# Twenty-nine input loads go out of ScalarE's DMA queue, a pair's turned r is copied at once, and every list of the schedule is new

## The chip, the cores and the metric

The kernel runs on one core of one Trainium2 chip. The metric is the device time of one execution in microseconds (us), the median of several runs. The core has five engines that run side by side, each working through its own list of instructions in order: TensorE (PE, matmul), VectorE (DVE), ScalarE (ACT), GpSimd (POOL) and SyncE (SP), which here only issues DMAs. Sixteen DMA engines move data between HBM and SBUF. TensorE writes to PSUM, which has eight banks.

## The reference

Two stages, one after the other. The first is a linear attention with a state per head (batch 4, 8 heads, 768 tokens, head size 40):

```python
for t in range(S):
    y[:, :, t] = np.einsum('bhd,bhde->bhe', rt, state)
    Sa = np.einsum('bhde,bhe->bhd', state, at)
    state_decay = state * wt[:, :, None, :] - np.einsum('bhd,bhe->bhde', Sa, bt)
    state = state_decay + np.einsum('bhd,bhe->bhde', vt, kt)
```

The second mixes tokens and channels of x, which is y with its heads side by side (4 x 768 x 320):

```python
theta = x @ w_theta
zr, zi = x * np.cos(theta), x * np.sin(theta)
y = np.einsum('ts,bsd->btd', w_tok_r, zr) + np.einsum('ts,bsd->btd', w_tok_i, zi)
u = x + y
return u + np.maximum(u @ w_ch, 0.0)
```

## The kernel before

**Tiling.** The tokens are cut into chunks of 128: six chunks a batch, 24 in all, named i = 0 to 23. Within a chunk the recurrence is turned into matrix products over the 128 tokens, with all 8 heads side by side (320 columns). Each chunk needs six inputs of 160 KB: w, k, b, a, v and r. `loads` (lines 433 to 449) issues them: one DMA a chunk for w, k, b and a (line 436), one for v from chunk 8 on, and two DMAs a pair of chunks for r, and for v below chunk 8 (line 448). These are 144 DMAs, and SP issues all of them in the kernel before.

**A chunk's stages.** `prep` takes ln(w) on ACT (line 472), sums it over the tokens on PE, takes exponentials on ACT (496, 506, 514), scales k, b and a by them on POOL (line 456, tiles kb and ah), and turns kb, ah, v and r (token to feature) on PE, by `turned` (lines 404 and 408) and `turn_runs` (569 and 572). A turned tile goes to PSUM and is copied to SBUF on ACT or DVE (lines 422 and 426 for most; 584 and 586 for r). `scores` (603, 612, 614) makes four 128 x 1024 score tiles a chunk, masked on DVE, or copied by ACT and masked on POOL. `recurrence` and `readout` follow (lines 640 to 842). `theta` and `sines` give cos and sin, `sines` multiplies them with x on POOL (line 894, zr and zi), `mix_row` does the token mixing (line 910: 288 matmuls of 320 columns), and `channels` the last product and the store (946, 949). Matrix weights are loaded by POOL (lines 961 and 989).

**Two ways to turn a tile.** In one bank: each 128 x 128 block is one transpose of 128 columns (lines 404, 569). In two banks: each block is two transposes of 64 rows and 64 columns, one for the upper and one for the lower half of the partitions, each into its own bank (lines 408, 572). `split` tells which of the two a tile has; the copies out of PSUM read the same number of elements either way.

**What sets the order.** Every step is an operation in a `Plan`, numbered in the order in which the program adds it. The list `ORDER` says in which order all are issued, and thereby each engine's own order. An operation can have a second variant: on another engine, or for a turned tile the one in two banks; `PICK` names the operations that take it. `HOMES` gives, in that order, the PSUM bank of each tile. `WARM` puts matmuls on constant data ahead of a few operations. The lists are constants of the program. Waits follow from the data: an engine waits at an operation until what it reads is there and what it overwrites has been read, and everything behind it in that engine's list waits too.

**A pair's r.** `turn_runs` turns r of two chunks in one PSUM tile. Before, two ACT copies of 128 x 256 words take it out, one a chunk (lines 581 to 588, 24 copies in all).

Of the kernel before, what the change touches and what calls it, by code (L numbers as in the profile page):

```python
# [9 lines left out]
FP32 = mybir.dt.float32  # L10
# [209 lines left out]
def kernel(  # L220
# [14 lines left out]
    nc = tc.nc  # L235
# [840 lines left out]
```

## Time and profile before

| | before |
|---|---|
| time, median of 3 runs | 197.25 us (196.4, 197.25, 198.79) |
| span of the profiled execution, first to last instruction | 195.9 us |
| PE / DVE / ACT / POOL busy | 94% / 83% / 77% / 74% of the span |
| granted TensorE clock, mean | 0.997 |
| first issue of an input load / issue of the last one | 0.81 us / 151.8 us |

The profile's span leaves out what lies ahead of the first and behind the last instruction; the three runs lie 0.5 to 2.9 us above it, their median 1.35 us. A PE that is busy all the time may still not be at its peak, since the ends of matmuls are modelled.

### The profile page before, as it was taken

To read this page: it belongs to the slowest core of one execution; us is meant where nothing else is said; L and a number is where in the kernel's file an instruction comes from. 1 tells how busy PE (TensorE), PEld (TensorE's weight loads), DVE (VectorE), ACT (ScalarE), POOL (GpSimd) and SP (SyncE) were. 2 spreads that over 40 slices of the span, in tenths; PEclk is the share of its full clock that TensorE was granted. 3 is DMA by queue.
4 is the path that set the end of the run, shared out by engine and by line. 5 is a ranking of instruction groups with operands and counts; after the bars stand their busy time and mean duration, and the time that the engine had idled before them with its cause. 6 is when DMAs were issued, how large, how long until landed. Compare 5 with 4: busy or idle time off the path is not lost.

```text
span 195.9 us, 8473 instructions
## 1 busy us (share of the span) xinstructions
PE 184.3 (94%) x3516; PEld 145.4 (74%) x3516; DVE 163.3 (83%) x260; ACT 150.6 (77%) x336; POOL 145.1 (74%) x211
## 2 busy tenths in 40 slices
PE   7889899999997999999899999999999999999992
PEld 6767687887786778887577787887788768767661
DVE  5378799999998999898897999999999938664453
ACT  3575879799997997999689599979999867575111
POOL 8367466579969999696699959868879997469100
PEclk9999999999999999999999999999999999999998
DMA  5999897999999999979999997789899977535055
GB/s 118 217 205 182 148 214 157 174 171 206 216 183 166 197 180 185 225 122 200 179 183 158 166 200 129 164 147 180 161 178 203 168 172 102 128 136 74 32 197 172
DMA packets 134646, 32.78 MB, mean 167 GB/s; under 512 B 124816, under 2 KB 134608, under 8 KB 134608
## 3 DMA queue, kind: packets, MB, share of 16 engines
q1 hardware_dynamic: 131680, 29.19, 76.6%
q0 software_dynamic: 2784, 2.97, 9.3%
q8 instruction: 27, 0.44, 0.9%
q10 hardware_dynamic: 144, 0.08, 0.1%
q14 instruction: 11, 0.09, 0.1%
HBM read 29.54 MB, written 3.93 MB: 171 GB/s over the span
## 4 chain that ended last, share of the span: by engine, by line
PE 61%; DMA 12%; POOL 9%; ACT 6%; DVE 4%; SPq 4%; issue 2%; ACTq 0%; DVEq 0%; POOLq 0%
PE banks L910 16%; PE banks L603 9%; PE banks L404 8%; PE banks L792 5%; DMA raw_a<-in_a_dram 4%; DMA raw_kb<-in_k_dram 4%; SPq L436 3%; PE banks L408 3%; DMA uT<-up 2%; PE banks L569 2%; PE banks L663 2%; POOL kb L456 2%; PE banks L686 2%; PE banks L802 2%; DMA raw_v<-in_v_dram 2%
## 5 line engine op out<-in xcount | busy, mean ns | idle before, releaser
L456 POOL TENSOR_TENSOR kb<-raw_kb,ex 128x320 bf16<-128x320 f32 x46 | 37.1, 814 | 8.0 <-DMA raw_kb<-in_k_dram 3.0
L910 PE MATMUL banks<-zr,wtok_r 128*128 128x320 bf16 x144 | 41.0, 300 | 0.2
L910 PE MATMUL banks<-zi,wtok_i 128*128 128x320 bf16 x144 | 40.8, 299 | 0.1
L456 POOL TENSOR_TENSOR ah<-raw_a,we 128x320 bf16<-128x320 f32 x22 | 19.0, 865 | 12.9 <-ACT we L506 4.7
L612 DVE TENSOR_TENSOR lamu<-banks,mask_p 128x1024 bf16<-128x1024 f32 x22 | 26.8, 1219 | 1.5 <-PE banks L603 0.8
L612 DVE TENSOR_TENSOR psi<-banks,mask_p 128x1024 bf16<-128x1024 f32 x22 | 26.8, 1219 | 0.8 <-PE banks L603 0.7
L612 DVE TENSOR_TENSOR phi<-banks,mask_n 128x1024 bf16<-128x1024 f32 x18 | 21.9, 1216 | 1.6 <-POOL r L462 1.3
L612 DVE TENSOR_TENSOR lamv<-banks,mask_p 128x1024 bf16<-128x1024 f32 x17 | 20.7, 1219 | 1.6 <-PE banks L603 1.0
L894 POOL TENSOR_TENSOR zi<-cs,xp 128x320 bf16<-128x320 f32 x22 | 17.2, 791 | 2.0 <-ACT cs L879 1.2
L910 PEld LDWEIGHTS <-wtok_r 128*128 128x128 bf16 x144 | 14.0, 97 | 5.6 <-issue 0.3
L603 PE MATMUL banks<-aT,kbT 64*128 64x128 bf16 x384 | 17.2, 217 | 0.9 <-DVE kbT L426 0.3
L894 POOL TENSOR_TENSOR zr<-cs,xp 128x320 bf16<-128x320 f32 x22 | 17.4, 802 | 0.1
L910 PEld LDWEIGHTS <-wtok_i 128*128 128x128 bf16 x144 | 14.0, 98 | 3.8 <-issue 0.3
L829 PE MATMUL banks<-kb,lamv 128*128 128x40 bf16 x192 | 14.9, 180 | 0.0
L831 PE MATMUL banks<-kb,lamu 128*128 128x40 bf16 x192 | 14.8, 179 | 0.0
L603 PEld LDWEIGHTS <-kbT 64*128 64x128 bf16 x384 | 11.8, 94 | 3.7 <-ACT kbT L422 1.1
L829 PEld LDWEIGHTS <-lamv 128*128 128x128 bf16 x192 | 13.2, 96 | 0.4
L916 DVE TENSOR_TENSOR up<-banks,xp 128x320 bf16<-128x320 f32 x22 | 10.6, 485 | 3.1 <-PE banks L910 2.9
L831 PEld LDWEIGHTS <-lamu 128*128 128x128 bf16 x192 | 13.0, 96 | 0.0
L472 ACT ACTIVATE lw<-raw_w 128x320 bf16<-128x320 f32 x24 | 11.5, 477 | 1.5 <-DMA raw_w<-in_w_dram 1.3
L496 ACT ACTIVATE ex<-banks 128x328 f32<-128x328 f32 (+1 forms) x24 | 10.8, 450 | 2.2 <-PE banks L491 1.1
L822 PE MATMUL banks<-gd,rT 128*128 128x80 bf16 x80 | 12.2, 197 | 0.0
(202 smaller groups left out, 583.0 us busy)
## 6 DMA issues: line engine op xcount, KB each, us to landing
raw_w<-in_w_dram SPq DMA_DIRECT2D x24, 160.0 KB, 4.3
raw_v<-in_v_dram SPq DMA_DIRECT2D x24, 160.0 KB, 3.7
raw_a<-in_a_dram SPq DMA_DIRECT2D x24, 160.0 KB, 3.9
raw_kb<-in_k_dram SPq DMA_DIRECT2D x24, 160.0 KB, 4.2
raw_kb<-in_b_dram SPq DMA_DIRECT2D x24, 160.0 KB, 4.2
raw_r<-in_r_dram SPq DMA_DIRECT2D x24, 160.0 KB, 3.8
out_dram<-oo SPq DMA_DIRECT2D x9, 160.0 KB, 2.6
wrow_i<-in_moe_w_tok_i_dram POOLq DMA_DIRECT2D x6, 192.0 KB, 5.3
```

What stands on the lines that cost most here:

```text
L404: nc.tensor.transpose(out=t[:, m * 128:m * 128 + 128], in_=src, identity=ident)
L456: pool = ("POOL", lambda: nc.gpsimd.tensor_tensor(out=dst, in0=in0, in1=in1, op=ALU.mult))
L472: add("ACT", "ln", i, lambda: nc.scalar.activation(out=paired(lw)[:, :, :, 0:D], in_=paired(raw_w[s4]), func=AF.Ln), 473, [("raw_w", s4)], ...
L496: got = add("ACT", "exp", i, lambda: nc.scalar.activation(out=ex[:, :, 0:D] if no_total else ex.rearrange("p h x -> p (h x)"), in_=sums(ps ...
L603: nc.tensor.matmul(t[:, q, g, :], lhsT=lhs[g][rows(q)], rhs=rhs[g][rows(q)], start=True, stop=True)
L612: add("DVE", kindm, i, lambda: nc.vector.tensor_tensor(out=flat, in0=whole(), in1=mask.to_broadcast([128, 2 * G, 128]), op=ALU.mult), 1217 ...
L822: nc.tensor.matmul(t[:, g * 80:g * 80 + 80], lhsT=by_two(rT)[g], rhs=gd[:, 2 * g:2 * g + 2, :], start=True, stop=False, skip_group_check=True)
L829: nc.tensor.matmul(o, lhsT=lamv[:, p, g, :], rhs=kb[:, 0, h, 0:D], start=first, stop=False, skip_group_check=True)
L831: nc.tensor.matmul(o, lhsT=lamu[:, p, g, :], rhs=kb[:, 1, h, 0:D], start=False, stop=True, skip_group_check=True)
L894: pool = ("POOL", lambda: nc.gpsimd.tensor_tensor(out=dst, in0=in0, in1=in1, op=ALU.mult))
L910: nc.tensor.matmul(acc(), lhsT=wtok[nm][j][:, s], rhs=zs[c][:, s], start=n == 0 and c == 0, stop=n == NT - 1 and c == 1)
L916: add("DVE", "uadd", q, lambda: nc.vector.tensor_tensor(out=u, in0=acc(), in1=x, op=ALU.add), 488, [pk, x_key(q)], [u_key(q)], at="row")
```

## The change

Three edits to the program, and new lists.

1. `loads` gives each of the 144 load operations a second variant, the same DMA issued by ACT (`nc.scalar.dma_start`).
2. In `turn_runs`, the two ACT copies of a pair's r become one of 128 x 512 words that writes both chunks' halves. There are 12 operations fewer (1602 become 1590), so all numbers behind them shift.
3. `ORDER`, `HOMES`, `PICK` and `WARM` are new as a whole.

Decoded against the numbering of the operations, the new lists say this (i in brackets):

| | before | after |
|---|---|---|
| loads issued by ACT | 0 | 29: a x9 (0, 4, 10, 11, 13, 14, 15, 17, 19), w x8 (1, 3, 4, 5, 6, 8, 17, 20), b x4 (1, 9, 17, 20), early v x3, k x2 (6, 8), r x2 (0), v x1 (17) |
| tiles kb turned in two banks | 8 of 23 | 21 of 23 (new: 0 to 5, 8, 9, 10, 12, 15, 21, 22) |
| nu | 2 of 22 | 12 of 22 |
| ah / v, early v, v back | 7, 5 | 10, 7 |
| u and x, feature-major | 1 and 5 | 7 and 9 |
| r (of 12) | 6 | 8 |
| turned tiles in two banks, all | 39 | 79 |
| planned operations: ACT / DVE / POOL / SP | 326 / 235 / 186 / 180 | 339 (29 of them loads) / 237 / 189 / 151 |

Of the ACT operations that change sides: copies of kb on DVE go from 7 to 4 and of ah from 8 to 5, copies `nx` on DVE from 4 to 8, early v from 0 to 4; casts of v on ACT go from 5 to 2 (POOL 11 to 14); z products on DVE from 2 to 6 (POOL 46 to 42); score tiles on ACT are 17 before, 18 after. The first chunks' loads of ACT stand in its list between its early operations: `la0, ln0, lw1, r, ew0, exp0, r, ea0, lb1, ln1, ...`. `lk8` stands ahead of `ln8`, `la13` ahead of the copy `ekb12`. At `spsi8`, `spsi13`, `spsi16` and `spsi23` (the first score of those chunks) PE has 0, 24, 48 and 90 of its 144 pairs of token-mixing matmuls behind it in the old order, 0, 24, 48 and 93 in the new one; at `y23`, the last readout, 106 in both.

```diff
@@ loads
         for key, dst, src in load(i):
-            add("SP", "l" + key[0][4:], i,
-                lambda dst=dst, src=src: nc.sync.dma_start(out=dst, in_=src),
-                600, [], [key], work=1030)
+            by = [(e, lambda q=q, dst=dst, src=src: q.dma_start(out=dst, in_=src))
+                  for e, q in (("SP", nc.sync), ("ACT", nc.scalar))]
+            add("SP", "l" + key[0][4:], i, by[0][1], 600, [], [key], work=1030, alts=(by[1],))
...
-                add("SP", "load" + nm, i, lambda c=c, to=raw[s], runs=runs: nc.sync.dma_start(
-                    out=to[:, c], in_=runs[c]), 600, [], [run_key(nm, i, c)], work=520)
+                by = [(e, lambda q=q, c=c, to=raw[s], runs=runs: q.dma_start(
+                    out=to[:, c], in_=runs[c])) for e, q in (("SP", nc.sync), ("ACT", nc.scalar))]
+                add("SP", "load" + nm, i, by[0][1], 600, [], [run_key(nm, i, c)], work=520,
+                    alts=(by[1],))
@@ turn_runs
-        for x, (dst, dkey) in enumerate(dsts):
-            if nm != "r":
+        if nm != "r":
+            for x, (dst, dkey) in enumerate(dsts):
                 evac("ACT", "e" + nm, i + x, pr, dst, 512, [dkey], x)
-                continue
-
-            def words(x=x, dst=dst):
-                out = dst.bitcast(FP32)
-                if split(pr):
-                    nc.scalar.copy(out=out, in_=ps(pr)[:, x, 0:256])
-                    return
-                nc.scalar.copy(out=out.rearrange("p (a n) -> p a n", a=2), in_=ps(pr).rearrange(
-                    "p (a n) -> p a n", a=2)[:, :, 128 * x:128 * x + 128])
-            add("ACT", "e" + nm, i + x, words, 512, [pr], [dkey])
+            return
+        both = rT_t[i // 2 % 3].rearrange("p x n -> p (x n)").bitcast(FP32)
+
+        def words():
+            if split(pr):
+                nc.scalar.copy(out=both.rearrange("p (x n) -> p x n", x=2), in_=ps(pr)[:, :, 0:256])
+                return
+            nc.scalar.copy(out=both.rearrange("p (x a n) -> p x a n", x=2, a=2),
+                           in_=ps(pr).rearrange("p (a x n) -> p x a n", a=2, x=2))
+        add("ACT", "er", i, words, 512, [pr], [dkey for _, dkey in dsts])
@@ the lists
-WARM = {21: (0, 25), 30: (1, 4), 33: (2, 1), 28: (1, 8), 41: (1, 11)}
+WARM = {21: (5, 25), 33: (1, 1), 30: (3, 4), 28: (5, 8), 41: (0, 11)}
...
```

249 rows, old and new, of tables (HOMES, ORDER, PICK) are left out of this document.

## The prediction

> **What bounds the kernel now.** I read the page's busy line first, then the windows (busy time in stretches of the span), the chain that ended last, and SP's timeline.
>
> ```profile
> span 195.9 us, 8473 instructions
> PE 184.3 (94%) x3516; PEld 145.4 (74%) x3516; DVE 163.3 (83%) x260; ACT 150.6 (77%) x336; POOL 145.1 (74%) x211
> ...
> PE 61%; DMA 12%; POOL 9%; ACT 6%; DVE 4%; SPq 4%; issue 2%; ACTq 0%; DVEq 0%; POOLq 0%
> ```
>
> PE is busy 94% of the span and makes 61% of the chain, but the whole is no single limit. The windows show it, with start and end, length, busy time of PE, PE's weight loads, DVE, ACT and POOL (instructions), the granted clock, the DMA engines' share and GB/s:
>
> ```profile
> 0.00:20.00 20.00, 16.42 (x233) 13.68 (x235) 12.86 (x40) 10.98 (x25) 12.61 (x35) 1.00 0.93 182
> 20.00:40.00 20.00, 19.14 (x396) 15.63 (x392) 18.18 (x22) 16.72 (x44) 11.28 (x14) 1.00 0.89 175
> 40.00:60.00 20.00, 18.61 (x384) 15.11 (x382) 19.61 (x25) 18.70 (x45) 16.99 (x25) 1.00 1.04 192
> 60.00:80.00 20.00, 19.53 (x440) 15.82 (x442) 18.93 (x27) 18.00 (x41) 19.78 (x29) 1.00 1.04 183
> 80.00:100.00 20.00, 19.30 (x420) 14.88 (x413) 17.86 (x27) 17.58 (x36) 14.97 (x22) 1.00 1.00 175
> 100.00:120.00 20.00, 19.77 (x391) 15.50 (x390) 18.06 (x31) 16.74 (x39) 17.91 (x25) 1.00 0.93 170
> 120.00:140.00 20.00, 19.98 (x504) 16.27 (x502) 19.53 (x28) 18.38 (x44) 16.19 (x22) 1.00 0.89 166
> 140.00:155.00 15.00, 14.82 (x325) 12.29 (x322) 14.61 (x22) 14.44 (x35) 13.92 (x19) 1.00 0.94 188
> 155.00:170.00 15.00, 14.79 (x235) 11.14 (x233) 10.74 (x18) 10.01 (x17) 11.94 (x16) 1.00 0.76 128
> 170.00:185.00 15.00, 14.91 (x165) 10.48 (x164) 7.42 (x14) 7.63 (x15) 9.55 (x12) 1.00 0.38 93
> 185.00:196.00 11.00, 7.07 (x63) 4.64 (x61) 5.55 (x13) 1.39 (x4) 0.00 (x0) 0.93 0.47 164
> ```
>
> Three stages. Up to 100 us PE is idle 7.0 us in all (3.58, 0.86, 1.39, 0.47, 0.70) while the DMA engines are 89 to 104% busy (a share over 1 means that packets overlapped): input loads lead. From 100 to 155 us PE, DVE, ACT and DMA are all near full and PE is idle 0.4 us of 55. From 155 us on only PE is full, down to the last stores. The clock is granted in full, so it plays no part. The chain says the same of the first stage (start, length, what):
>
> ```profile
> 48.22 7.07 DMA raw_kb<-in_k_dram
> ...
> 82.25 2.88 SPq L436
> ...
> 86.11 8.33 DMA raw_a<-in_a_dram
> 94.58 0.88 POOL ah L456
> ...
> 95.50 0.29 PE banks L408 x8
> ```
>
> Two loads, k of chunk 8 and a of chunk 13, take 7 and 8 us and hold POOL, and behind it PE. In the new lists both are among the 29 of ACT.
>
> **The tiles turned in two banks.** This is the surest term. Groups by line and shape, PE matmuls (count | busy us, mean ns):
>
> ```profile
> L404 PE MATMUL banks<-wide,kb 128*128 128x128 bf16 x120 | 9.8, 225 | 1.0 <-ACT phi L614 0.7 <-POOL kb L456 0.3
> L404 PE MATMUL banks<-wide,ah 128*128 128x128 bf16 x64 | 6.4, 224 | 0.0
> L569 PE MATMUL banks<-wide,r 128*128 128x128 bf16 x48 | 3.7, 219 | 0.0
> L408 PE MATMUL banks<-wide,kb 64*128 64x64 bf16 x128 | 3.2, 191 | 0.2 <-ACT uT L422 0.2
> L572 PE MATMUL banks<-wide,r 64*128 64x64 bf16 x96 | 2.4, 190 | 0.0
> L408 PE MATMUL banks<-wide,ah 64*128 64x64 bf16 x56 | 2.0, 192 | 1.2 <-POOL ah L456 1.2
> L404 PE MATMUL banks<-wide,xp 128*128 128x128 bf16 x20 | 1.8, 218 | 0.0
> L408 PE MATMUL banks<-wide,xp 64*128 64x64 bf16 x50 | 1.6, 190 | 0.0
> ```
>
> A whole kb is 8 matmuls: 120 are 15 tiles, 9.8/15 = 0.65 us of PE each. In two banks it is 16: 128 are 8 tiles, 3.2/8 = 0.40. So a kb tile that changes saves 0.25 us. In the same way ah: 6.4/16 - 2.0/7 = 0.11; r: 3.7/6 - 2.4/6 = 0.22; x (5 blocks): 1.8/4 - 1.6/5 = 0.13. nu and v have ah's four blocks and are priced as ah, u as x, early v as r. By the decoded lists: kb +13 tiles, 3.3 us; nu, ah, v together +14 (10, 3 and 1), 1.5; u and x +10, 1.3; r and early v +3, 0.7. That is 6.8 us of PE. It isn't 6.8 us of time. By chunk numbers only three kb (15, 21, 22; 0.75), three tiles net of nu, ah and v (0.33), some nine of u and x (1.2) and one r (0.2) fall behind about 95 us, where PE is the engine that ends last: 2.4 us, taken in full. The other 4.4 lie where loads lead; they shorten links of the chain but mostly make PE wait longer. I take a fifth, **0.9** (bounds 0 and 4.4), beside the **2.4**. What hides the rest is the load stream; if that gets faster, more of the 4.4 counts. The price in banks: 40 more tiles hold two of the eight banks. No row shows PE waiting long for a bank; the kb row's 0.7 us behind an ACT copy (phi, of another tile) is nearest. I take nothing, with 2.8 us (four such waits) as the other end.
>
> **The 29 loads.** What an issue costs its engine, by SP's timeline (start, length), first to last load:
>
> ```profile
> 0.81 0.46 SPq L436 DMA_DIRECT2D raw_w<-in_w_dram  x1
> ...
> 24.92 0.53 SPq L436 DMA_DIRECT2D raw_kb<-in_k_dram  x1
> ...
> 90.50 3.70 SPq L436 DMA_DIRECT2D raw_kb<-in_b_dram  x1
> ...
> 151.08 1.34 SPq L448 DMA_DIRECT2D raw_r<-in_r_dram  x2
> ```
>
> SP issues without a pause: 144 loads and 3 stores in 151.6 us, 1.03 us each; a free issue takes 0.53, the slowest 3.70. The long ones come when SP's queue is full of transfers that the DMA engines haven't done, since these are 89% busy and more. ACT's queue would hold a fifth as many, so I price its issues near the free end, at 0.58: 29 x 0.58 = 16.8 us of ACT. Nothing in the trace shows a load on ACT; the bounds are 0.46 and 1.03 a piece, 3.70 for single ones. From 20 to 155 us ACT is idle 14.4 us, and about 20 of the 29 lie there (11.6 us), so it fits, with little left. Behind an issue in ACT's list stand copies out of PSUM for which PE waits; ACT makes 6% of the chain, so I charge 6% of 14.7 (16.8 less 2.1 saved below): **0.9 us lost**, with the rival below as the other end.
>
> What it gains: the two loads of the chain no longer stand behind SP's full queue. PE is idle 1.39 us in the stretch that holds the first wait and 0.70 in that of the second; I take half of the 2.1, **1.0**, since neither idle time is all due to them; bounds 0 and 2.1.
>
> The Trainium skill (DMA: Bandwidth & Descriptors, Issuing engines are not separate DMA queues) says that DMAs of SP, ACT and GpSimd run on the same 16 engines and that issuing from several saves issue time only. By it this 1.0 would be nothing, and the sum 195.5 us. The same page (Queues, rings and completion order) has each DMA engine go round between the queues that have work, packet by packet; by that a load on a nearly empty queue overtakes those of a full one, which speaks for the 1.0. No run here shows two loading queues yet.
>
> **The copy of r.**
>
> ```profile
> L422 ACT COPY kbT<-banks 128x512 f32<-128x512 f32 x12 | 7.1, 592 | 2.6 <-PE banks L404 2.5
> L586 ACT COPY rT<-banks 128x256 f32<-128x256 f32 x12 | 4.4, 384 | 0.2 <-PE banks L569 0.2
> L584 ACT COPY rT<-banks 128x256 f32<-128x256 f32 x12 | 4.1, 382 | 0.8 <-PE banks L572 0.8
> ```
>
> Two copies of 0.383 become one that has the size of kbT's, 0.592: 0.174 saved a pair, 2.1 us of ACT over 12. The even chunk's half is ready 0.21 us later, the odd one's 0.17 earlier. ACT doesn't end last; nothing on the path, beyond the 2.1 already set against the issues.
>
> **Work that changes engine, and the order.** Without loads ACT goes from 326 to 310 operations, of which 12 are the copies of r. DVE gets 2 more, POOL 3. At DVE's mean of 0.63 us (163.3/260) that is 1.3 us; DVE is 98% busy in 120 to 140 us, so I count half, **0.6 us lost**; POOL, 74% busy, hides its three. The new order keeps the old shape (the token mixing stands 0 to 3 pairs further at the same chunks); I give it no term.
>
> **Sum.** -2.4 - 0.9 - 1.0 + 0.9 + 0.6 = -2.8 us, 195.9 to 193.1 us of span. The median of the runs is 1.35 us above the profiled span, so about **194.5 us**, 1.4% below 197.25.
>
> **Rivals.**
>
> *The load stream stays the floor (chance 0.27).* The same 144 loads move the same bytes through DMA engines that are 89 to 104% busy until 155 us. Then all that PE saves before turns into waiting for loads, and only what lies behind 155 us counts: about seven of the changed tiles, 0.8 us, 196.4 us. The Trainium skill's rule on issuing engines (same page and section as above) leads to this case too. For it: the DMA share. Against: from 100 to 140 us it is 0.89 to 0.93, so there is some room, and a second queue that always has work can use it.
>
> *ACT becomes the bound (0.16).* If issues on ACT take what SP's do, 1.03 us, the 20 behind 20 us cost 20.6, less 1.9 for the r copies: 18.7 against 14.4 us of idle time up to 155 us. ACT then ends last, 4.3 us late: 201.5, and with copies that PE waits for about 202 us (199.5 to 205). It decides where the mean issue passes (14.4 + 1.9)/20 = 0.82 us. For it: SP's mean, and that one full DMA side may hold up both queues. Against: SP's free issues.
>
> *The second queue opens the first stage (0.17).* Early loads land sooner, the two waits go, and most of the 4.4 us of PE time and the whole 2.1 count: 3.5 + 1.1 beyond my sum is 189.9 us at best; two thirds of that way is 191.5 (189.5 to 193). For it: PE's 7.0 us of idle time before 100 us, and a chain that there runs through loads and POOL. Against: the first 20 us already move 182 GB/s.
>
> The forecast has the remaining 0.40, with a range of its own of 192 to 197.
>
> **Range and chances.** 190.5 to 199.8 holds all but the far part of ACT's case (about 0.12) and the edge of the fast one (0.05). What can be told from no change is about 2%: 193.3 and 201.2. Faster: the fast case, 0.17, and a third of the forecast's 0.40, together 0.31. Slower: some two thirds of ACT's case, 0.11, and 0.03 for bank waits beyond 2.8 us: 0.14. Within: 0.55.
>
> **What would show it.** Right: L408 kb at x336 and about 8.4 us, L404 kb at x16; ACTq load issues of about 0.6 us; waits of POOL for k and a under 2 us each; PE idle below 6 us in the first 100. ACT's idle time in 20 to 155 us should fall to some 5 us. The floor's case: the last load lands where it did and PE is idle longer between 40 and 155 us. ACT's case: issues over 0.82 us, and PE waiting for copies of ACT. Wrong altogether: PE waiting for banks, or chunk 0 later than before.

## The result, and the profile after

The changed kernel is slower: 208.16 us (median of four, 207.04 to 210.18) against 196.85 us of the kernel before on the same chip, a ratio of 1.053 with a 95% interval of 1.047 to 1.059. The forecast was 194.5 us, with a range up to 199.8. Ratios here compare undisturbed executions only; where the times of one kernel spread more than that, its range is given beside them.

The page after, with the lines that answer to those of before: span, busy time of the engines, and the chain that ended last by engine.

```profile
span 206.6 us, 8911 instructions
...
PE 183.9 (89%) x3744; PEld 142.4 (69%) x3744; DVE 164.7 (80%) x262; ACT 148.0 (72%) x320; POOL 148.1 (72%) x214
...
PE 47%; DMA 15%; POOL 8%; SPq 8%; ACT 8%; DVE 7%; issue 4%; ACTq 1%; DVEq 0%; POOLq 0%
```

PE is busy as long as before (183.9 us against 184.3), but the span is 10.7 us longer: the loss is time in which PE waits. The windows show where. The columns are start and end, length, busy time of PE, weight loads, DVE, ACT and POOL, granted clock, DMA share and GB/s.

```profile
0.00:20.00 20.00, 11.56 (x143) 9.67 (x144) 6.35 (x30) 5.56 (x11) 11.49 (x34) 1.00 1.03 188
20.00:40.00 20.00, 18.96 (x460) 14.79 (x458) 18.41 (x26) 16.77 (x39) 11.93 (x15) 1.00 1.04 187
...
60.00:80.00 20.00, 18.14 (x338) 14.25 (x337) 16.61 (x23) 15.93 (x36) 15.95 (x23) 0.91 1.07 184
80.00:100.00 20.00, 19.51 (x487) 15.38 (x485) 17.16 (x27) 18.83 (x41) 18.39 (x27) 1.00 1.18 206
100.00:120.00 20.00, 18.33 (x377) 13.59 (x370) 18.88 (x32) 14.89 (x29) 18.32 (x25) 1.00 0.66 127
120.00:140.00 20.00, 17.79 (x440) 14.14 (x440) 16.63 (x24) 16.32 (x39) 13.60 (x19) 1.00 1.03 187
```

Three stretches have lost PE time against before: the first (11.56 us busy instead of 16.42), 60 to 80 us (18.14 instead of 19.53), and 100 to 140 us (36.12 instead of 39.75). In the first two the DMA engines are at least as full as before. In 100 to 120 us they are not: 0.66 instead of 0.93. So two things are to be explained.

**The first: ACT stands still ahead of its own load issues.** ACT's timeline after (start, length, engine, line; ACTq is a DMA issue of ACT; in brackets the idle time before and what ended it):

```profile
5.87 0.44 ACT L503 ACTIVATE ex<-banks 128x328 f32<-128x328 f32 x1
8.21 0.54 ACTq L453 DMA_DIRECT2D raw_r<-in_r_dram  x1
8.79 0.37 ACT L431 COPY aT<-banks 128x256 f32<-128x256 f32 x1 [2.48 <-PE banks L413]
13.85 0.41 ACTq L440 DMA_DIRECT2D raw_kb<-in_b_dram  x1
14.30 0.47 ACT L479 ACTIVATE lw<-raw_w 128x320 bf16<-128x320 f32 x1 [5.14 <-DMA raw_kb<-in_b_dram]
```

The issues are short (0.54 and 0.41 us). But between the copy at 8.79 and the issue at 13.85 ACT does nothing for 4.7 us, and ln(w) of chunk 1 stands behind that issue. The timeline says that this ln(w) waited for a landing of `raw_kb`, a tile that it does not read. That contradiction is the clue: what waits is the DMA issue ahead of it. In the trace each DMA of SP or ACT reports its landing on one of eight semaphores (counters that an engine can wait for), which all of them share, 22 or 23 DMAs on each, whichever engine issues. Ahead of 23 of ACT's 29 issues the trace has a wait for the issue's own semaphore, so the earlier DMA on it has to land first. For b of chunk 1 that was SP's load of b of chunk 2: it landed at 13.825 us by the trace's semaphore events, and ACT's issue began 0.02 us later. Eleven of the 29 issues began within 0.1 us of such a landing. The chain that ended last goes through four of them, right behind a landing; two of the four (start, length, what):

```profile
12.87 3.16 DMA raw_r<-in_r_dram
16.05 0.55 ACTq L453
16.64 0.45 ACT ex L503
...
114.50 5.28 DMA raw_r<-in_r_dram
119.86 0.37 ACTq L440
120.27 0.59 ACT rT L591
```

Here an ACT operation on the path waits for a load that it has nothing to do with. Added up over the 29 issues, ACT stands idle 14.4 us ahead of them (4.68, 2.58, 1.90, 1.89 and 1.00 the largest). PE has its longest wait behind the first of these (what waits, for what, us in all, times, longest):

```profile
PE banks L510 <- ACT lw L479: 5.1, 1, 5.1
```

**The second: SP halts.** SP's timeline after:

```profile
100.29 0.60 SPq L440 DMA_DIRECT2D raw_kb<-in_k_dram  x1
111.78 0.55 SPq L453 DMA_DIRECT2D raw_r<-in_r_dram  x1
```

SP issues nothing for 10.9 us. The new order puts the first load of r of pair 18 right behind k of chunk 15; its buffer is that of pair 14 (two buffers), and POOL's cast of r of pair 14 ends at 111.75. In the kernel before, SP never stood over 0.9 us ahead of a load. The late load of pair 18's other half, issued at 114.50, is the one in the chain above that ACT then waits for.

The delay against before does not grow evenly: it is 4.9 us at chunk 0's first score (10.7 before, 15.5 after), falls to 3.6 by chunk 7, is 7.0 at chunk 8, 5.4 at chunk 13, 8.7 at chunk 16 and 10.4 at chunk 23. So PE makes up a part in between, and loses again behind the waits of 60 to 80 and 100 to 140 us.

### The profile page after: what moved, and what is told of

Read it like the earlier page. It is cut to its first block, busy times and chain, and to the rows that moved or that the text cites. A ratio compares the mean times of both kernels' runs of the same rounds, so it can differ in the third digit from the quotient of the medians.

```text
span 206.6 us, 8911 instructions
## 1 busy us (share of the span) xinstructions
PE 183.9 (89%) x3744; PEld 142.4 (69%) x3744; DVE 164.7 (80%) x262; ACT 148.0 (72%) x320; POOL 148.1 (72%) x214
## 4 chain that ended last, share of the span: by engine, by line
PE 47%; DMA 15%; POOL 8%; SPq 8%; ACT 8%; DVE 7%; issue 4%; ACTq 1%; DVEq 0%; POOLq 0%
PE banks L917 10%; DMA raw_r<-in_r_dram 8%; PE banks L610 7%; SPq L440 7%; PE banks L799 4%; PE banks L413 4%; PE banks L409 4%; DMA wch<-in_moe_w_ch_dram 3%; DMA raw_w<-in_w_dram 2%; POOL zr L901 2%; DMA uT<-up 2%; PE banks L693 2%; PE banks L670 2%; ACT cs L886 2%; PE banks L651 1%
## 5 line engine op out<-in xcount | busy, mean ns | idle before, releaser
L463 POOL TENSOR_TENSOR kb<-raw_kb,ex 128x320 bf16<-128x320 f32 x48 | 38.5, 812 | 9.9 <-ACT ex L503 8.3
L619 DVE TENSOR_TENSOR psi<-banks,mask_p 128x1024 bf16<-128x1024 f32 x23 | 28.0, 1219 | 10.2 <-PE banks L610 9.4
L619 DVE TENSOR_TENSOR phi<-banks,mask_n 128x1024 bf16<-128x1024 f32 x17 | 20.7, 1220 | 1.0 <-PE banks L610 0.6
L901 POOL TENSOR_TENSOR zi<-cs,xp 128x320 bf16<-128x320 f32 x20 | 16.1, 819 | 6.1 <-ACT cs L886 3.9
L619 DVE TENSOR_TENSOR lamv<-banks,mask_p 128x1024 bf16<-128x1024 f32 x16 | 19.5, 1217 | 0.7 <-PE banks L610 0.7
L610 PE MATMUL banks<-aT,kbT 64*128 64x128 bf16 x384 | 18.6, 223 | 0.8 <-ACT vT L427 0.8
L901 POOL TENSOR_TENSOR zr<-cs,xp 128x320 bf16<-128x320 f32 x19 | 15.5, 830 | 1.8 <-ACT cs L886 1.8
L708 POOL TENSOR_TENSOR gt<-sum,ex 128x320 bf16<-128x320 f32 x13 | 9.6, 739 | 9.8 <-DVE sum L704 8.6
L923 DVE TENSOR_TENSOR up<-banks,xp 128x320 bf16<-128x320 f32 x22 | 10.4, 485 | 4.5 <-PE banks L917 4.2
```

What stands on the lines that cost most here:

```text
L463: pool = ("POOL", lambda: nc.gpsimd.tensor_tensor(out=dst, in0=in0, in1=in1, op=ALU.mult))
L610: nc.tensor.matmul(t[:, q, g, :], lhsT=lhs[g][rows(q)], rhs=rhs[g][rows(q)], start=True, stop=True)
L619: add("DVE", kindm, i, lambda: nc.vector.tensor_tensor(out=flat, in0=whole(), in1=mask.to_broadcast([128, 2 * G, 128]), op=ALU.mult), 1217 ...
L708: add("POOL", "wgt", i, lambda: nc.gpsimd.tensor_tensor(out=new_state, in0=sum_t, in1=wm.to_broadcast([128, 8, D]), op=ALU.mult), 830, [(" ...
L901: pool = ("POOL", lambda: nc.gpsimd.tensor_tensor(out=dst, in0=in0, in1=in1, op=ALU.mult))
L923: add("DVE", "uadd", q, lambda: nc.vector.tensor_tensor(out=u, in0=acc(), in1=x, op=ALU.add), 488, [pk, x_key(q)], [u_key(q)], at="row")
```

## The experiments

Operations are numbers in the lists. `PICK` entries set to 1 give an operation its second variant: a load on ACT, a tile in two banks. All times are compared with the kernel before on the same chip.

**All loads back on SP**, the new order kept. The 29 load numbers leave `PICK`:

```diff
 PICK = {
-    3: 1, 4: 1, 5: 1, 8: 1, 10: 1, 18: 1, 19: 1, 25: 1, 26: 1, 27: 1, 28: 1, 30: 1, 32: 1, 33:
+    25: 1, 26: 1, 27: 1, 28: 1, 30: 1, 32: 1, 33: 1, 34: 1, 35: 1, 36: 1, 37: 1, 39: 1, 40: 1,
...
```

> The changed kernel with its 29 ACT loads issued by SP again, at the same places of the order; all else as changed. Theory A (the trace after shows ACT starting a load 20 ns after the landing of an earlier DMA on the same completion semaphore, with nothing behind it running meanwhile): nearly all of the 11 us come back, 194 to 198 us, chunk 0's first score near 10.7 us again instead of 15.5. Rival B (the new order, banks and two-bank tiles are at fault): 204 us or more. Not told apart at 199 to 203.

203.4 us, ratio 1.024 (1.015 to 1.033). About half of the loss goes and half stays, between the two expectations: the loads on ACT are not the whole cause, and the new order costs something without them. Chunk 0's first score is back at 10.4 us. SP's halt is gone as well, although the order is the same: SP has 29 issues more and comes to the load of pair 18 at 109.27 us, 0.1 us behind its issue before, when the cast of pair 14 has just ended (108.94). So this run takes away both ACT's waits and the halt, and the halt belongs to the loads on ACT: with fewer issues of its own SP is earlier at a buffer that isn't free yet.

**The first nine ACT loads back on SP** (nine numbers leave `PICK`: a of chunk 0, w of 1, 3 and 4, b of 1, both loads of r of pair 0 and of v of pair 2):

```diff
 PICK = {
-    3: 1, 4: 1, 5: 1, 8: 1, 10: 1, 18: 1, 19: 1, 25: 1, 26: 1, 27: 1, 28: 1, 30: 1, 32: 1, 33:
+    25: 1, 26: 1, 27: 1, 28: 1, 30: 1, 32: 1, 33: 1, 34: 1, 35: 1, 36: 1, 37: 1, 39: 1, 40: 1,
...
```

> The changed kernel with only the first nine of its ACT loads (those ahead of chunk 3) issued by SP, 20 still by ACT. Theory A: the 5 to 7 us that chunks 0 to 2 are late after the change come back, 201 to 204 us, and the loss behind 55 us stays. If the early loss is made up later anyway (PE has waits there), 206 to 208. Rival B: 207 to 209, chunk 0 still late.

209.9 us, 1.051 (1.038 to 1.064): nothing gained. Chunk 0's first score comes at 10.0 us, as early as before. But the next ACT loads now wait instead: w of chunk 5 2.47 us (k of chunk 4 landed at 27.255, the issue began at 27.28), a of chunk 4 1.57, and w of chunk 20 2.49 where it was 1.00. The sum is 12.6 us of ACT, little less than 14.4. Taking off the loads that waited did not take off the waiting.

**The old order with the same 29 loads on ACT**, the second variant added to `loads` as in the change:

```diff
 PICK = {
-    25: 1, 31: 1, 37: 1, 39: 1, 40: 1, 48: 1, 49: 1, 75: 1, 80: 1, 85: 1, 86: 1, 115: 1, 118: 1,
+    3: 1, 4: 1, 5: 1, 8: 1, 10: 1, 18: 1, 19: 1, 25: 1, 31: 1, 37: 1, 39: 1, 40: 1, 48: 1, 49:
...
```

> The kernel before, its own order, banks and variants, with the same 29 loads issued by ACT at their places in the old order. Theory A: slower than before by as much as the change or more, 203 to 212 us, ACT standing at issues for 10 us or more in all. Rival B: 196 to 199 us, since an issue costs ACT 0.4 to 0.6 us and ACT has idle time.

215.2 us, 1.085 (1.077 to 1.093): worse than the change itself, and 3 us beyond what my own theory gave. ACT's idle time ahead of its issues is 13.5 us, and the chunks' first scores are 9.8 us late from chunk 1 on and 16 to 17 from chunk 8 on. The mean granted clock was 0.956 (0.997 in the kernel before) and PE was busy 188.1 us instead of 184.3, so a part of the loss is slower matmuls behind the waits. The loads on ACT alone are enough for the loss, in an order with none of the new tiles and none of the new places of loads. The longest wait on ACT's timeline:

```profile
10.57 0.59 ACT L424 COPY kbT<-banks 128x512 f32<-128x512 f32 x1
16.86 0.39 ACTq L437 DMA_DIRECT2D raw_kb<-in_b_dram  x1
19.02 0.54 ACTq L450 DMA_DIRECT2D raw_v<-in_v_dram  x1
19.61 1.02 ACT L618 ACTIVATE phi<-banks 128x1024 bf16<-128x1024 f32 x1 [8.46 <-DMA raw_kb<-in_b_dram]
```

**The old order with one copy of r a pair**, as the change has it:

```diff
+        if nm != "r":
+            for x, (dst, dkey) in enumerate(dsts):
                 evac("ACT", "e" + nm, i + x, pr, dst, 512, [dkey], x)
...
+            return
...
+        add("ACT", "er", i, words, 512, [pr], [dkey for _, dkey in dsts])
```

> The kernel before with a pair's turned r copied at once, at the place of the first of the two copies. Both theories: 196 to 198 us, no difference; ACT busy about 2 us less (12 copies of some 0.59 us for 24 of 0.383).

198.2 us, 1.000 (0.995 to 1.005): no difference, as forecast. ACT's busy time fell by 0.8 us (150.6 to 149.8) where I expected 2.

**Only three loads on ACT, in the old order** (the second variant added likewise): b of chunk 1 and both halves of v of pair 2, the ones around the 8.46 us above.

```diff
 PICK = {
-    25: 1, 31: 1, 37: 1, 39: 1, 40: 1, 48: 1, 49: 1, 75: 1, 80: 1, 85: 1, 86: 1, 115: 1, 118: 1,
+    10: 1, 18: 1, 19: 1, 25: 1, 31: 1, 37: 1, 39: 1, 40: 1, 48: 1, 49: 1, 75: 1, 80: 1, 85: 1,
...
```

> The kernel before with only three loads on ACT, in their old places of the order: b of chunk 1 and both halves of v of pair 2 (these stood 5.7 and 2.2 us behind landings of SP's loads when all 29 were moved). Theory (ACT stands still at an issue until an earlier transfer that uses the same completion semaphore has landed): ACT is idle 5 to 8 us between 10 and 20 us and everything behind is later by as much: 202 to 206 us. Rival (the number of issues is what costs, 0.4 to 0.6 us of ACT each): 196.5 to 198.5 us.

204.1 us, 1.036 (1.029 to 1.042). Three issues of 1.6 us together cost 7 us of time:

```profile
9.18 0.58 ACT L422 COPY kbT<-banks 128x512 f32<-128x512 f32 x1
14.18 0.45 ACTq L435 DMA_DIRECT2D raw_kb<-in_b_dram  x1
15.48 0.61 ACTq L448 DMA_DIRECT2D raw_v<-in_v_dram  x1
16.14 1.02 ACT L616 ACTIVATE phi<-banks 128x1024 bf16<-128x1024 f32 x1 [6.38 <-DMA raw_kb<-in_k_dram]
18.73 0.54 ACTq L448 DMA_DIRECT2D raw_v<-in_v_dram  x1
```

Each issue begins 0.02 us after SP's load on the same semaphore has landed (b of chunk 2 at 14.156, k of 2 at 15.458, r of pair 2 at 18.708). From chunk 1 to chunk 7 the first scores are 8.2 us late, to a tenth; 6.6 of it are still there at chunk 23. Behind PE's 6.3 us without work the granted clock was 0.50 for 10.2 us; what of the 8.2 is the clock's this run does not separate, and the next one bounds it.

**The same three loads on ACT, issued earlier**: in `ORDER` they stand right behind b of chunk 0, so they are ACT's second to fourth work.

```diff
 ORDER = [
-    0, 7, 3, 6, 1, 20, 2, 21, 8, 23, 24, 4, 27, 32, 9, 30, 22, 33, 31, 25, 5, 34, 26, 12, 28,
+    0, 7, 3, 6, 1, 20, 2, 10, 18, 19, 21, 8, 23, 24, 4, 27, 32, 9, 30, 22, 33, 31, 25, 5, 34,
...
```

> The kernel before with the same three loads on ACT that cost 7 us in the last experiment (b of chunk 1 and both halves of v of pair 2), now issued right behind ACT's first operation, where only six loads stand ahead of them and no earlier transfer has used their semaphores. Theory (the wait for the earlier transfer on the same semaphore is what costs, not the issue and not the engine): no idle time of ACT ahead of these issues, 196.5 to 199.5 us; up to 2 us may go to chunk 0's own loads, which now share the DMA engines with them. Rival (a load on ACT costs as such, by what it does to the queues or to ACT): 202 to 206 us, as there.

198.5 us, 1.004 (1.000 to 1.009). The trace has no wait ahead of these issues, and the first runs while ACT computes:

```profile
3.52 0.47 ACT L474 ACTIVATE lw<-raw_w 128x320 bf16<-128x320 f32 x1 [1.43 <-DMA raw_w<-in_w_dram]
3.52 0.44 ACTq L435 DMA_DIRECT2D raw_kb<-in_b_dram  x1
4.00 1.33 ACTq L448 DMA_DIRECT2D raw_v<-in_v_dram  x2
5.38 0.44 ACT L508 ACTIVATE we<-banks 128x320 f32<-128x320 f32 x1 [1.40 <-PE banks L505]
```

In the profiled execution chunk 1 stands 3.0 us late, of which 1.4 is left at chunk 23: its w landed later (ACT's ln(w) at 10.60 us had waited 2.36 us for it), and the granted clock was 0.50 from 7.3 to 17.5 us, as long as in the run above. The same three DMAs on the same engine, 7 us at one place and under 2 at another: it is the wait for the earlier transfer, not the engine, not the issue and not the clock.

**Twenty of the 29 on ACT, in the old order**: those ahead of whose issue ACT had hardly been idle when all 29 were there.

```diff
 PICK = {
-    25: 1, 31: 1, 37: 1, 39: 1, 40: 1, 48: 1, 49: 1, 75: 1, 80: 1, 85: 1, 86: 1, 115: 1, 118: 1,
+    3: 1, 8: 1, 25: 1, 31: 1, 37: 1, 39: 1, 40: 1, 48: 1, 49: 1, 53: 1, 75: 1, 80: 1, 85: 1, 86:
...
```

> The kernel before with 20 of the 29 loads on ACT, in their old places: those ahead of whose issue ACT was not idle (or under 0.1 us, the first one apart) when all 29 were moved. Theory (only issues that have to wait cost): 20 issues of 0.4 to 0.6 us are 8 to 12 us of ACT, of which a small part shows, besides up to 3 us of waits that turn up anew now that compute stands earlier against the loads: 197 to 202 us. Rival (cost by the number of loads, 18 us for 29): 207 to 211 us.

208.4 us, 1.053 (1.046 to 1.060). My number missed and the rival's fits, but the trace does not show a cost by the number of loads. Of the 8.7 us that ACT stands idle ahead of its issues, 8.6 lie at three, 6.17 us at 21.06, 0.92 at 54.18 and 1.51 at 74.62 us. The delay of the first scores goes up around them, to 7.2 us at chunk 3, 8.8 at chunk 7 and 10.6 at chunk 10, and stays at 10.2 to 10.6 to the end, although ten more issues of ACT follow. SP also halts for 9.92 us, up to 111.53, ahead of a load of w whose buffer ACT's ln(w) frees, and the delay does not change: a halt of SP is not lost time by itself. The first of the three issues stands in the chain:

```profile
16.56 4.48 DMA raw_kb<-in_k_dram
21.06 0.41 ACTq L436
21.52 0.59 ACT kbT L423
```

This is w of chunk 3, whose wait had been none with 29 loads on ACT. Whether an issue waits is no property of that load: with other loads on ACT the eight semaphores fall to other transfers. This is also why taking off the first nine gained nothing.

**The loads of r of pair 18 moved behind k of chunk 19 and a of chunk 20**, all else as in the changed kernel (1004 and 1005 are the two loads):

```diff
-    816, 484, 1024, 817, 978, 965, 956, 818, 979, 931, 1004, 929, 1025, 950, 485, 1028, 932,
...
+    1019, 1056, 1087, 830, 1013, 831, 1057, 1050, 1004, 1095, 1256, 1127, 1063, 1096, 1058,
+    1064, 832, 1059, 833, 1052, 1065, 1104, 1005, 834, 1060, 1038, 1014, 1035, 1066, 1067, 1257,
...
```

> The kernel after with one edit: the two loads of r of pair 18 stand behind k of chunk 19 and a of chunk 20 in the order instead of right behind k of chunk 15; the 29 loads stay on ACT. Theory (SP's 10.9 us halt at that load, which waits for POOL's cast of r of pair 14, is time of the whole): SP doesn't halt there, the DMA share of 100 to 120 us rises from 0.66 to about 0.9, and the ACT waits behind SP's late loads (2.6 us at b of chunk 17, 1.0 at w of chunk 20) shrink: 203.5 to 206.5 us. Rival (the loads behind the halt had slack of 20 us and more, so it is harmless): 207.3 to 209.5 us.

205.3 us, 1.043 (1.035 to 1.050). SP no longer halts 10.9 us in one place but twice, 4.55 us ahead of w of chunk 18 and 5.55 ahead of k of chunk 18, each until the last reader of that buffer is done. The DMA share of 100 to 120 us is 0.85, and the ACT waits at b of chunk 17 and w of chunk 20 are gone (the one at v of chunk 17 grew from 0.44 to 1.49):

```profile
99.87 1.40 SPq L440 DMA_DIRECT2D raw_v<-in_v_dram  x1
105.83 0.37 SPq L440 DMA_DIRECT2D raw_w<-in_w_dram  x1
...
109.03 0.98 SPq L440 DMA_DIRECT2D raw_v<-in_v_dram  x1
115.56 1.14 SPq L440 DMA_DIRECT2D raw_kb<-in_k_dram  x2
```

From chunk 15 on the first scores stand 3.5 to 4.5 us earlier than in the changed kernel. But 1.2 to 1.7 us of that is there from chunk 8 on, ahead of the moved loads, so the edit brought some 2 us, as the ratios say (1.053 to 1.043, with intervals that overlap at their edges). The halt at this load was a part of the loss, small against its length.

**All loads on SP, sorted by need**: each behind the last reader of its buffer, then by the time of its first reader in the trace of the first experiment.

```diff
 ORDER = [
-    0, 6, 7, 3, 1, 2, 20, 8, 21, 12, 5, 23, 32, 24, 22, 9, 33, 4, 27, 34, 35, 25, 30, 36, 31,
+    0, 6, 7, 3, 1, 2, 20, 8, 21, 12, 4, 23, 32, 24, 22, 5, 33, 9, 27, 34, 35, 25, 30, 36, 31,
...
```

> The kernel after with all loads on SP, as in the first experiment (203.4 us), and SP's loads sorted by the time of their first reader in that experiment's trace, each behind the last reader of its buffer; every other operation in the place it has after. Theory (what is left of the loss is SP's order of the loads: a of chunk 4, r of pair 6, w of chunk 9 land just before they are needed): PE's idle time before chunk 4's and pair 6's turns (2.1 and 1.3 us) goes: 199 to 201.8 us. Rival (the order of the casts and copies on POOL, ACT and DVE is what costs, whatever the loads do): 202.3 to 205 us.

201.4 us (198.45 to 203.04), 1.011 (1.000 to 1.021; the interval overlaps with that of the first experiment). PE's idle times before chunk 4's and pair 6's turns are gone, and the first scores of chunks 0 to 8 stand 0 to 1.4 us earlier than in the kernel before. In the profiled execution, one of the longer ones, 3.75 us of PE then go in one place. VectorE, then PE:

```profile
101.54 4.97 DVE L898 TENSOR_TENSOR zr<-cs,xp 128x320 bf16<-128x320 f32 x1
106.44 0.88 DVE L921 TENSOR_TENSOR up<-banks,xp 128x320 bf16<-128x320 f32 x2
...
107.37 0.29 PE L411 MATMUL banks<-wide,nu 64*128 64x64 bf16 x8 [3.75 <-DVE up L921]
```

The turn of nu waits for a bank that DVE empties with `up`, and DVE is held 4.97 us by one product of zr, which the change moved from POOL to DVE.

**The same once more**: sorted by this run's trace (22 loads move by one or two places), and o of pair 0 copied by ACT as before.

```diff
 ORDER = [
-    0, 6, 7, 3, 1, 2, 20, 8, 21, 12, 4, 23, 32, 24, 22, 5, 33, 9, 27, 34, 35, 25, 30, 36, 31,
+    0, 6, 7, 3, 1, 2, 20, 8, 21, 5, 12, 23, 32, 24, 22, 4, 33, 9, 27, 34, 35, 25, 30, 36, 31,
...
```

> The kernel after with all loads on SP, sorted by need a second time (by the trace of the first such run; 22 loads change places, by one or two), and o of pair 0 copied by ACT as before instead of POOL. Theory (with the loads off ACT and in the order of need, the new order is as good as the old, and the two-bank tiles are a gain of about 1 us): 195.5 to 198.5 us, level with before or 1% better. Rival (the new order of the other operations still costs 1 to 2%): 199 to 202 us.

201.8 us, from 196.3 to 204.7 in twelve executions; the shortest of them give a ratio of 1.001 (0.996 to 1.007), the median of all is 1.9% over the 198.06 of before. The same zr product takes 5.03 us in the profiled one.

**That product back on POOL**, all else as in the first sorted kernel:

```diff
 PICK = {
...
-    788: 1, 801: 1, 819: 1, 842: 1, 865: 1, 883: 1, 885: 1, 906: 1, 913: 1, 914: 1, 927: 1, 929:
+    788: 1, 819: 1, 842: 1, 865: 1, 883: 1, 885: 1, 906: 1, 913: 1, 914: 1, 927: 1, 929: 1, 931:
...
```

> The kernel with all loads on SP and sorted by need (201.4 us, 198.5 to 203.0), with one more edit: the third zr/zi operation of chunk 11, which the change gives to DVE, is POOL's again as before. In that kernel's trace it took DVE 4.97 us at 101.54 us, while POOL ran seven operations without a pause, and PE stood idle 3.75 us behind it. Theory (that wait is what lengthens most of its executions): the long times go, 195.5 to 198.5 us with a spread of under 2 us, level with before or up to 1% faster. Rival (the rest of the new order costs, and that operation only took over a wait that would come anyway): 199.5 to 202.5 us.

201.2 us, from 197.7 to 205.4 in twelve executions (the shortest give a ratio of 1.002, 0.998 to 1.007; the median of all is 1.8% over before): the theory falls. The profiled execution (199.47 us) has no such operation any more, and from chunk 13 to 19 its first scores stand within 1 us of the kernel before. But the spread is as wide as it was, so that product is not what lengthens most executions. What does stays open.

**One bank again**: the first experiment's kernel (all loads on SP) with the 49 newly split tiles whole.

```diff
 PICK = {
-    25: 1, 26: 1, 27: 1, 28: 1, 30: 1, 32: 1, 33: 1, 34: 1, 35: 1, 36: 1, 37: 1, 39: 1, 40: 1,
+    25: 1, 26: 1, 27: 1, 32: 1, 34: 1, 35: 1, 37: 1, 39: 1, 40: 1, 50: 1, 51: 1, 73: 1, 74: 1,
...
```

> The kernel after with all loads on SP, and the 49 tiles that the change turns in two banks (13 kb, 11 nu, 6 a, 12 x and u, 7 others) back in one. By the forecast's prices that adds about 7.8 us of PE work, some 2.7 of it late and taken in full, a fifth of the rest besides: 206 to 208.5 us against the first experiment's 203.4. Rival one (in this order PE mostly waits for others, or two banks cost as much in waits for banks as they save): 201.5 to 204.5 us. Rival two (PE is bound almost everywhere, all 7.8 count): 210 to 212 us.

204.3 us, 1.037 (1.030 to 1.045), and a span of 201.7 instead of 200.3. PE's busy line, of this kernel and then of the first experiment's:

```profile
PE 186.6 (93%) x3476; PEld 145.3 (72%) x3476; DVE 164.6 (82%) x262; ACT 148.8 (74%) x320; POOL 148.2 (73%) x214
```

```profile
PE 182.6 (91%) x3744; PEld 140.4 (70%) x3744; DVE 165.2 (82%) x262; ACT 148.7 (74%) x320; POOL 148.2 (74%) x214
```

PE is busy 4.0 us less with the 49 tiles in two banks, not the 7.8 that the forecast's prices add up to, and the span is 1.4 us shorter in these two executions (0.9 between the medians, 2.6 between the ratios, whose intervals overlap). The 4.0 is too low as a price: from 36.4 to 39.8 us the kernel in two banks had a granted clock of 0.50 while PE was busy without a pause, and the kernel in one bank had the full clock up to 200 us. At the first scores of chunks 1 to 8, where loads lead, the kernel in one bank is even 0.3 to 1.8 us ahead; at those of chunks 15 to 20 it is 0.8 to 1.5 us behind.

## Why the prediction was wrong

**The step that failed is the price of the 29 issues**: "I price its issues near the free end, at 0.58", and then "ACT makes 6% of the chain, so I charge 6% of 14.7". The size of the issue was right, even high: the mean of the 29 is 0.42 us. What was left out, and so put at nothing without a reason, is what an issue waits for before it begins. That an engine's list runs in order, and that all behind a waiting instruction waits too, stood in the description of the kernel; but as things to wait for it named only what an operation reads and overwrites, and not the earlier transfer that uses the same semaphore. SP's rows hid it: SP's issues follow one another about 0.05 us apart, and in the kernel before each began at least 2.0 us after the earlier landing on its semaphore, so these waits were over, and SP has no compute behind them. With the halt of SP that they bring, the 29 loads on ACT cost 5 to 6 us in the new order (the step from 1.053 to 1.024) and 16.8 us in the old one (8.5% of 198). The edit whose price I spread over a share of the chain stood on the chain itself at four of its issues, each right behind a landing.

The reason given for SP's long issues, a full queue, is borne out only in part: in the trace of the kernel before an issue took 0.58 us on average with none of SP's earlier transfers outstanding (issued and not landed), 0.85 to 0.98 with one to four and 1.30 with five, but the longest, 3.70, came with three.

**The rival of ACT as the bound** named the right engine and the wrong rule. It was to decide at a mean issue of 0.82 us; the mean stayed at 0.42 and the time passed 202 all the same. ACT's busy time did not grow (148.0 us): it was idle, 18.7 us of 20 to 155 us where I expected some 5.

**The gain of 1.0 ("the two loads of the chain no longer stand behind SP's full queue")** did not come. POOL's waits for k and a did fall under 2 us, so the two waits went. But POOL's longest waits for kb are now for ACT, 8.3 us in three places:

```profile
POOL kb L463 <- ACT ex L503: 8.3, 3, 4.5
...
ACT lw L479 <- DMA raw_kb<-in_b_dram: 5.1, 1, 5.1
```

The columns are the time waited in all, how often, and the longest. The wait for a load was passed on by way of ACT. The rule of the Trainium skill weighed there (DMA: Bandwidth & Descriptors, Issuing engines are not separate DMA queues) says that a second issuing engine saves issue time only. By it the term was nothing, and no gain shows in the runs, but neither the rule nor I had the loss. The Trainium skill says in another section of that page (Anatomy of one DMA — SWDGE (gpsimd) path) that a semaphore wait is done by the issuing sequencer before it dispatches. The traces agree for ACT's queue, with issues that begin 0.02 us after a landing. I did not put the two together.

**"I give it no term"**, said of the new order, failed as well. With all loads on SP the new order is 2.4% slower than the old, in spite of its cheaper turns; sorting the loads alone brings the median from 203.4 to 201.4, though the intervals of the two ratios overlap. I compared how far the token mixing had moved and not where each load stands against the last reader of its buffer and against its first reader. That the load of pair 18 stands behind k of chunk 15, and that its buffer's last reader is the cast of pair 14, was readable from the new lists. That SP would halt there was not, from the lists alone: with all loads on SP the gap at this load is 0.1 us.

**The tiles in two banks** were the term of the right kind and too large. L408's kb row was forecast at x336 and 8.4 us, with x16 left whole:

```profile
L413 PE MATMUL banks<-wide,kb 64*128 64x64 bf16 x336 | 8.8, 195 | 0.7 <-DVE xp L845 0.4 <-ACT lamv L621 0.3
...
L409 PE MATMUL banks<-wide,kb 128*128 128x128 bf16 x16 | 1.2, 219 | 0.0
```

8.8 and 1.2 (against 3.2 and 9.8 before) save 3.0 us where I had 3.3. Between the one-bank kernel and its counterpart the turns' rows fall by 7.5 us, close to the 7.8 of the prices, while other matmul groups grow by 2.4, at least in part through the stretch at half clock, and PE's busy time falls by 4.0. So the price of a tile was about right, and what was too large is the share that I took as time: of the forecast 3.3 us some 0.9 to 2.6 came. PE waiting for banks, the other end of 2.8 us, did not show beyond 0.7 us in a row of these tiles in the changed kernel; in the first sorted kernel it did once, 3.75 us at the turn of nu shown above.

**The copy of r**: nothing on the path, right; ACT saved 0.8 us of busy time by it, not 2.1. **DVE's two more operations, 0.6**: not measured alone; in the changed kernel the moved zr product takes 1.41 us.

**The other two rivals.** Two signs of the load stream as the floor came, a last load that was issued at 152.5 us (151.8 before) and more idle time of PE between 40 and 155 us, but it was to give 196.4 us, and a DMA share of 0.66 in 100 to 120 us is no stream at its limit. The second queue did not open the first stage: the first 20 us moved 188 GB/s instead of 182, and PE's idle time up to 100 us went from 7.0 to 12.7 us.

**"Wrong altogether: ... chunk 0 later than before"** is what happened, at 15.5 instead of 10.7 us, though through ACT and not through the banks or the DMA engines. Of the loss of 11.3 us the runs place about half at the loads on ACT, by ACT's waits and by the halt of SP (some 2 us) together, and about a quarter at the order of the loads, the last with overlapping intervals. The rest, 1 to 2%, belongs to executions of the sorted kernels that spread over nearly 8 us in the last run, where the kernel before spread over 3.6 on the same chip, and is not explained.

No version beats the kernel before.

## What to carry to other kernels

Before a DMA is moved to an engine that computes, ask what its issue will wait for: with the eight shared semaphores of this program an issue stands until an unrelated earlier transfer has landed, and everything behind it in that engine's list stands too. Here a second issuing engine was safe only where that semaphore was free (three early loads cost 0.4%, the same three a little later 3.6%), and an operation that waits for a tile it does not read points to such an issue ahead of it. When a schedule is replaced as a whole, read from the lists where each load stands against the last reader of its buffer, and ask how much earlier the first queue gets there when another takes over a part of its loads, before any gain of the parts is summed.

## What the runs showed of the hardware

An issue on ACT can begin while ACT's previous operation still runs: in the early variant above both start at 3.52 us. What held up the operations behind it was the wait of an issue for its semaphore, up to 6.2 us; the issues themselves took 0.37 to 1.84 us, the longest with 29 loads on ACT in the old order.

A product of two SBUF operands on DVE waits for POOL. By the ends in the traces each zr or zi product on DVE is done 0.34 to 0.37 us after the end of a POOL operation: the one of chunk 11 is 1.41 us long after the change, 1.70 with all loads on SP, 0.98 with one bank. In the two profiles where it took 4.97 and 5.03 us, POOL ran seven operations without a gap (this is POOL's timeline of the first):

```profile
102.05 0.78 POOL L899 TENSOR_TENSOR zi<-cs,xp 128x320 bf16<-128x320 f32 x1
102.78 0.44 POOL L467 CAST v<-raw_v 128x320 bf16<-128x320 f32 x1
103.19 1.56 POOL L461 TENSOR_TENSOR kb<-raw_kb,ex 128x320 bf16<-128x320 f32 x2
104.72 0.78 POOL L899 TENSOR_TENSOR zi<-cs,xp 128x320 bf16<-128x320 f32 x1
105.46 0.71 POOL L467 CAST r<-raw_r 128x640 bf16<-128x640 f32 x1
```

DVE's operation ended at 106.51, 0.35 us behind the last. The Trainium skill (SBUF — State Buffer, SBUF: two separate sides) describes a lock that the one engine holds for a whole instruction while the other waits; the traces agree for one instruction, and show besides that the waiting DVE can miss six ends in a row.

The granted clock fell to 0.50 for a while behind some of the stretches in which PE had stood idle: for 3.4 us from 65.1 us on in the changed kernel, behind 1.8 us without work, and for 10.2 us with three loads on ACT, behind 6.3 us. It did not behind all of them: in the changed kernel PE also stood idle for 5.1 us from 9.7 us on, and the clock stayed at 1.00. No run separates what that costs.
